# A Mamba-2 scan with an ELU feed-forward block: the second layer from Strassen products to 12-bit words, with the first layer's words kept in DRAM

## The chip, the cores and the metric

The kernel runs on one core of one Trainium2 chip. A core has TensorE (PE; its weight loads are shown as PEld), VectorE (DVE), ScalarE (ACT), GpSimd (POOL) and SyncE (SP, which here only issues transfers). The metric is the device time of one execution in microseconds (us); less is better.

## The reference

A chunked state-space scan gives 3072 rows of 256 values; these go through a feed-forward block of two layers, 256 to 2048 and back, with ELU between them.

```python
batch, n_heads, seq, head_dim, d_state = (4, 8, 768, 32, 16)
...
n_tokens, d_model, d_ff = (3072, 256, 2048)
...
    log_a = np.log(np.clip(a, 1e-06, 1.0))
...
        cum = np.cumsum(la, axis=-1)
        L = np.exp(cum[:, :, :, None] - cum[:, :, None, :])
        L = L * causal
        M = CB * L
        y_intra = np.einsum('bhij,bhjd->bhid', M, xc)
        y_inter = np.einsum('bhin,bhnd->bhid', Cc, state) * decay_to_i[:, :, :, None]
        y[:, :, sl] = y_intra + y_inter
...
    h = x @ w_in
    g = np.where(h > 0.0, h, alpha * (np.exp(np.minimum(h, 0.0)) - 1.0))
    return (g @ w_out).astype(np.float32)
```

The weights `w_in` and `w_out` arrive as 64-bit floats and are turned into 32-bit ones on the chip.

## The kernel before

The 3072 rows are 12 blocks of 256 rows (`BLK`). For each block the scan makes `yT` (the block's rows, transposed), the first layer makes 16 tiles of hidden values, and the second layer sums over these 16 into the block's output. The order of instructions on every engine is the order of the calls in the source (`manual_schedule`); an instruction that waits holds back all that stands behind it on its engine. Semaphores between engines follow from the tiles, and a tile of a pool takes a place that an earlier tile of its tag has left.

Blocks 0 and 1 and a half of the first layer of blocks 2 and 3 are computed with full 32-bit products (`l1` L669, `l2` L854). Everything behind that is done for two blocks at a time: a stage is one round of the loop at L1403 with n = 4, 6, 8, 10 (blocks n and n+1), and the loop at L1322 does the second half of the first layer of blocks 2 and 3. A stage has 16 steps k, one for each tile of 128 hidden values.

The first layer of a step (`l1_words`, L801) works on 12-bit words. Both factors are split into a high word and a rest (`words_of_w` L746, `low_of_w` L756, `words_of_y` L765, `both_of_y` L791), a product of words passes TensorE once per column, and three products give the result: high times high and low times low into `high`, and the product of the sums into `both`. That is six matmuls of 512 columns. ACT then scales `both` into `e` (L818), DVE adds `high` (L826), ACT takes relu and exp (`begin_end`, L832), and DVE writes the hidden values `g` at the beginning of the next step (`end_words`, L839). The words of `w_in` stay in SBUF for the whole run.

The second layer of a pair of blocks lags one stage behind (`second`, L900). It is one level of Strassen's scheme in Winograd's form, with full 32-bit products: seven products instead of eight, in two halves over the hidden dimension. The sums of weights (`weight_steps` L719, `differences` L1267) are made once; the sums of hidden values (`sum_t2` L892 and the `sub` calls on POOL) and the sums of products (`add` on DVE) are made in every stage. `second` is a generator; `l2s(count)` (L1407) draws `count` pieces of two matmuls from it, between the first-layer matmuls of the steps.

The last pair of blocks (10 and 11) has its second layer on words (`late_l2`, L1032): `w_out` is stored to DRAM in 32 bits (`keep_w` L736), read back when the scan's buffers are free (`late_pool` L976) and split, and the hidden values are split, by `jobs`, in the stage n = 10 and behind it. A job has three instructions: ACT takes the high word, DVE the low one, POOL (or DVE in the tail) their difference (`late_words_of_g`, L1000).

The scan of the next pair of blocks runs inside a stage. `stage_scan` (L1383) loads its inputs and makes the decays: `spread_cum` (L387) has loaded the running sums of a block into `L` (128 x 8 x 2 x 64), and `decay_of` (L528) takes, for each head and half, an exponent on ACT with a bias (128x64), 32 for a pair of blocks; after every four heads POOL sets what is above the diagonal to zero (`affine_select`). In step 9 the scores are multiplied with `L` (`weigh` L557) and the states advance (`states` L588), in step 13 the outputs of the scan are made (`across`, `inside`), and at the end of a stage the words of the new `yT` are made ahead of its first step.

PSUM has eight places of one bank: seven of tag "a", and one of tag "o".

Of the kernel before, what the change touches and what calls it, by code (L numbers as in the profile page):

```python
# [23 lines left out]
DIRECT = 4  # L24

# [7 lines left out]
def kernel(  # L33
# [49 lines left out]

    def psum(shape, name):
        return p_a.tile(shape, F32, tag="a", name=name)
# [5 lines left out]
    first = ffn.tile([P, 4, 2, P], F32, tag="c", name="first", bufs=1)  # L91
# [6 lines left out]
    la = const.tile([ROWS, 2, P], F32, name="la")  # L98
# [59 lines left out]
    for i in w_order:  # L158
        w_in[i] = conv.tile([P, KC, CW], F32, tag="w_in", name="w_in", bufs=DF // CW + 1)
    w_out = const.tile([P, MC, DM], F32, name="w_out")  # L160
# [6 lines left out]
    for i in range(MC // 2):  # L167
        pieces.append((
            w_out[:, 2 * i:2 * i + 2],
            w_out64.rearrange("(m p) e -> p m e", p=P)[:, 2 * i:2 * i + 2]))  # L170
    w_raw = {}
    W_AHEAD = 11

    def w_load(i, parts=1):
        if i < len(pieces):
            w_raw[i] = conv.tile([P, 2, 2 * CW], U32, tag="w64", name="w64", bufs=W_AHEAD)
# [8 lines left out]
    w_mag, w_abs_of = {}, {}  # L185
# [4 lines left out]

    def w_abs(i, cols=slice(None)):
        if i in (1, 2) or cols.start:
            w_abs_of[i, cols.start] = psum([P, 2, CW], "ps_mag").bitcast(U32)
        if i not in w_mag:
            w_mag[i] = (ffn.tile([P, 2, CW], U32, tag="tmp", name="mag", bufs=1) if i == 2 else
                        ffn.tile([P, 2, CW], U32, tag="g0", name="mag", bufs=12))
# [17 lines left out]
    w_sgn = {}  # L214

    def w_sign(i, cols=slice(None), eng=nc.vector):
        if i not in w_sgn:
            w_sgn[i] = ffn.tile([P, 2, CW], U32, tag="g1", name="sgn", bufs=12)
# [88 lines left out]
    minus = const.tile([P, P], F32, name="minus")  # L307
# [214 lines left out]

    def decay(n, q):

        decay_of(n, 2 * q)
        decay_of(n, 2 * q + 1)
# [141 lines left out]

    def l1(n, i, parts=1):  # L669
# [22 lines left out]
    def elu():  # L692
        if not begun:
# [4 lines left out]
        g_of[n, i] = ffn.tile([P, 2, BLK], F32, tag=f"g{n % 2}", name="g", bufs=12)  # L698
        nc.vector.scalar_tensor_tensor(
            out=g_of[n, i], in0=e, scalar=1.0, in1=ps,  # L700
# [14 lines left out]
    def sum_weights(eng, a, s, i):  # L715
        for step in weight_steps(eng, a, s, i):
            step()

    def weight_steps(eng, a, s, i):  # L719
        a11, a12, a21, a22 = (part[:, i] for part in a)  # L720
        s2, _, s4 = (part[:, i] for part in s)
        for out, in0, in1, op in (
                (a21, a21, a22, ALU.add), (s2, a21, a11, ALU.subtract), (s4, a12, s2, ALU.subtract)):
            yield lambda: eng.tensor_tensor(out=out, in0=in0, in1=in1, op=op)

    def weight_sums():
        return [conv.tile([P, MC // 2, P], F32, tag="w64", name="w_sum", bufs=W_AHEAD)
                for _ in range(3)]

    w_parts = w_out.rearrange("p (i k) (r c) -> p k r i c", k=2, c=P)  # L730
    a_out = [w_parts[:, k, r] for r in range(2) for k in range(2)]
    s_out = []
    w_kept = tc.dram_tile([P, MC, DM], F32, name="w_kept")
    kept_parts = w_kept.rearrange("p (i k) (r c) -> p k r i c", k=2, c=P)

    def keep_w(k, r):  # L736
        nc.sync.dma_start(out=kept_parts[:, k, r], in_=w_parts[:, k, r])

# [3 lines left out]
    def words_of_w(i):  # L746

        w = pieces[i][0]
        k_words[i] = conv.tile(
            [P, 2, KC, CW], F32R, tag="w64", name="w_words", bufs=W_AHEAD)  # L750
# [5 lines left out]
    def low_of_w(i):  # L756

        w0 = conv.tile([P, KC, CW], F32R, tag="w_in", name="w0", bufs=DF // CW + 1)
# [42 lines left out]
    def l1_words(n, m, ahead=None):  # L801
# [17 lines left out]
        if n == NP - 2 and m > 1:  # L819
            first_of_job()  # L820
# [7 lines left out]
        if n == NP - 2 and m > 1:  # L828
            second_of_job()
# [9 lines left out]
    def end_words():  # L839
        n, m, h, e = late.pop(0)  # L840
        g_of[n, m] = ffn.tile([P, 2, BLK], F32, tag=f"g{m % 2}", name="g", bufs=12)
# [429 lines left out]
    for j in range(2 * DIRECT):  # L1271
# [45 lines left out]
        if j == 3:  # L1317
            s_out[:] = weight_sums()
# [185 lines left out]
```

## Time and profile before

| | us |
|---|---|
| median of 3 runs | 348.37 |
| lowest, highest | 347.66, 348.43 |
| the profiled execution | 348.77 |
| its span, first to last instruction | 347.0 |

The span has these parts, with TensorE's granted clock at 1.00 in all: up to about 20 us the first scan and the first weights; to 82 the blocks 0 and 1 and the 32-bit half of 2 and 3; to about 113 the other half; then the stages n = 4, 6, 8 of some 53 us each; the stage n = 10 up to 320; and the second layer of the last two blocks. HBM was read with 24.61 MB and written with 5.44 MB.

A row of the groups by shape gives line, engine, operation, the tile written and the tiles read, the shape, the count; then the busy time and the mean of one in ns; then the idle time of the engine ahead of them and what ended it. In the chain of waits and the timeline a row begins with the start and the length in us.

### The profile page before, as it was taken

Reading aid. Unit: us, or ns where it says so; the run is one execution under the profiler, and the core shown is the slowest. Engines: PE = TensorE matmul, PEld = TensorE weight load, DVE = VectorE, ACT = ScalarE, POOL = GpSimd, SP = SyncE. Lnnn points to the kernel's source line nnn. Section 1 sums busy time; section 2 is a strip of 40 time slices with the busy share of each in tenths; the row PEclk is TensorE's granted clock in tenths of the full one; section 3 lists DMA queues with packets and bytes.
Section 4 is the critical chain, followed back from the end, with each engine's and each line's share of the span. In section 5 each row is a group of like instructions: output and inputs, shape, how many; then the busy total and the mean of one; then the engine's idle time right before and its main releaser. Section 6 shows DMA issues by size and latency. Waiting matters only on the chain.

```text
span 347.0 us, 9962 instructions
## 1 busy us (share of the span) xinstructions
PE 339.5 (98%) x3902; PEld 297.7 (86%) x3902; DVE 275.3 (79%) x533; ACT 247.7 (71%) x563; POOL 215.8 (62%) x319
## 2 busy tenths in 40 slices
PE   8899999999999999999999999999999999999995
PEld 6569888888788899888889988889988989999995
DVE  3898998889997999866788775788685769898961
ACT  4798989599649988657599547499647487877601
POOL 5553554548999699975196864196954357787200
PEclk9999999999999999999999999999999999999999
DMA  8788999473360660160331070140003500000001
GB/s 146 199 234 177 281 198 257 86 153 97 74 139 2 159 184 23 17 154 4 95 73 30 9 160 5 66 72 2 2 2 89 219 0 3 0 2 30 33 0 62
DMA packets 77208, 30.70 MB, mean 88 GB/s; under 512 B 57897, under 2 KB 71529, under 8 KB 77161
## 3 DMA queue, kind: packets, MB, share of 16 engines
q1 hardware_dynamic: 74984, 29.86, 35.3%
q8 instruction: 31, 0.51, 0.6%
q10 hardware_dynamic: 2176, 0.20, 0.5%
q14 instruction: 17, 0.13, 0.1%
HBM read 24.61 MB, written 5.44 MB: 87 GB/s over the span
## 4 chain that ended last, share of the span: by engine, by line
PE 61%; DVE 12%; ACT 11%; POOL 5%; issue 5%; SPq 2%; DMA 2%; DVEq 0%; ACTq 0%; POOLq 0%
PE ps_o L924 16%; PE ps_h L812 11%; PE ps_h L677 11%; PE ps_o L861 6%; PE ps_w L812 6%; PE ps_both L1042 6%; DVE ps_h L826 4%; ACT e L834 4%; POOL g L877 3%; ACT e L835 3%; DVE y L786 2%; DMA w<-in_moe_w_in_dram 2%; ACT yT L661 2%; DVE M L560 2%; DVE y_both L796 1%
## 5 line engine op out<-in xcount | busy, mean ns | idle before, releaser
L834 ACT ACTIVATE e<-ps_h 128x512 f32<-128x512 f32 x72 | 43.0, 598 | 49.0 <-DVE ps_h L826 49.0
L842 DVE SCALAR_TENSOR_TENSOR g<-e,ps_h 128x512 f32<-128x512 f32 x72 | 49.3, 684 | 30.9 <-ACT e L835 29.1
L924 PEld LDWEIGHTS ps_o<-w_out,g 128*128 128x128 f32 x512 | 64.1, 191 | 5.3 <-ACT p_sum L936 1.1
L924 PE MATMUL ps_o<-w_out,g 128*128 128x128 f32 x512 | 66.3, 276 | 0.6 <-ACT p_sum L936 0.4
L826 DVE SCALAR_TENSOR_TENSOR ps_h<-ps_h,e 128x512 f32<-128x512 f32 x72 | 49.9, 693 | 10.1 <-ACT e L818 8.9
L812 PE MATMUL ps_w<-y_both,w_words 128*128 128x512 f32 x144 | 51.5, 437 | 0.1
L818 ACT ACTIVATE e<-ps_w 128x512 f32<-128x512 f32 x72 | 42.2, 586 | 10.8 <-PE ps_w L812 10.6
L835 ACT ACTIVATE e<-e 128x512 f32<-128x512 f32 x72 | 45.5, 631 | 2.3
L677 PE MATMUL ps_h<-yT,w_in 128*128 128x256 f32 (+1 forms) x208 | 45.2, 368 | 1.9 <-POOL w_in L249 1.9
L812 PE MATMUL ps_h<-y,w_words 128*128 128x512 f32 x144 | 45.6, 398 | 0.0
L877 POOL TENSOR_TENSOR g<-g 128x256 f32<-128x256 f32 x28 | 22.7, 811 | 36.2 <-DVE g L842 36.1
L812 PE MATMUL ps_h<-y,w 128*128 128x512 f32 x144 | 44.9, 392 | 0.0
L677 PEld LDWEIGHTS ps_h<-yT,w_in 128*128 128x128 f32 x208 | 36.3, 190 | 7.7 <-POOL w_in L249 2.8
L531 ACT ACTIVATE L<-L,ncum 128x64 f32<-128x64 f32 x160 | 42.2, 336 | 0.1
L536 POOL TENSOR_SCALAR_AFFINE_SELECT L<-L 64x512 f32<-64x512 f32 x40 | 29.4, 735 | 8.0 <-ACT L L531 6.7
L812 PEld LDWEIGHTS ps_h<-y,w 128*128 128x128 f32 x144 | 27.0, 188 | 7.0 <-POOL w L877 0.4
L924 PE MATMUL ps_o<-w_sum,g 128*128 128x128 f32 x256 | 32.8, 276 | 0.0
L924 PEld LDWEIGHTS ps_o<-w_sum,g 128*128 128x128 f32 x256 | 31.4, 191 | 1.4
L812 PEld LDWEIGHTS ps_h<-y,w_words 128*128 128x128 f32 x144 | 26.6, 188 | 6.1 <-issue 0.4
L861 PE MATMUL ps_o<-w_out,g 128*128 128x256 f32 x128 | 30.4, 381 | 0.0
L861 PEld LDWEIGHTS ps_o<-w_out,g 128*128 128x128 f32 x128 | 24.0, 190 | 3.5
L877 POOL TENSOR_TENSOR g<-t,g 128x256 f32<-128x256 f32 x32 | 23.1, 750 | 4.7 <-PE ps_o L924 4.7
(152 smaller groups left out, 667.4 us busy)
## 6 DMA issues: line engine op xcount, KB each, us to landing
L<-flat SPq DMA_DIRECT2D x20, 256.0 KB
w<-in_moe_w_out_dram SPq DMA_DIRECT2D x8, 512.0 KB
w<-in_moe_w_in_dram SPq DMA_DIRECT2D x7, 512.0 KB
xr<-in_x_dram SPq DMA_DIRECT2D x24, 128.0 KB
w_kept<-w_out SPq DMA_DIRECT2D x4, 512.0 KB
out_dram<-c_sum SPq DMA_DIRECT2D x8, 256.0 KB
w_again<-w_kept SPq DMA_DIRECT2D x4, 512.0 KB
bc<-in_B_dram SPq DMA_DIRECT2D x24, 64.0 KB
```

The source lines that it names most:

```text
L531: nc.scalar.activation(L[:, h, u], L[:, h, u], ACT.Exp, bias=ncum[:, u, row:row + 1])
L536: nc.gpsimd.affine_select(out=part, in_=part, pattern=[[0, 4], [0, 2], [1, Q]], compare_op=ALU.is_ge, fill=0.0, base=0, channel_multiplier=-1)
L677: nc.tensor.matmul(out=ps[:, j, toks], lhsT=w_in[i][:, k, j * P:(j + 1) * P], rhs=yT[n // 2][:, k, n % 2].rearrange("p u i -> p (u i)")[:, ...
L812: nc.tensor.matmul(out=ps, lhsT=lhs[:, k], rhs=rhs[:, k], start=k == 0 and lhs is not w0, stop=k == KC - 1 and lhs is not w1)
L818: nc.scalar.activation(e, both, ACT.Copy, scale=WORD)
L826: nc.vector.scalar_tensor_tensor(out=high, in0=high, scalar=WORD - 1.0, in1=e, op0=ALU.mult, op1=ALU.add)
L834: nc.scalar.activation(e, high, ACT.Relu, scale=-1.0)
L835: nc.scalar.activation(e, e, ACT.Exp, scale=-1.0)
L842: nc.vector.scalar_tensor_tensor(out=g_of[n, m].rearrange("p b i -> p (b i)"), in0=e, scalar=1.0, in1=h, op0=ALU.subtract, op1=ALU.max)
L861: nc.tensor.matmul(out=o_of[n][:, ts], lhsT=g_of[n, j][:, m % 2, ts * P:(ts + 1) * P], rhs=w_out[:, m], start=(m == 0 and ts == 0), stop=( ...
L877: nc.gpsimd.tensor_tensor(out=out, in0=in0, in1=in1, op=ALU.subtract)
L924: nc.tensor.matmul(out=ps[:, ts], lhsT=b[:, ts * P:(ts + 1) * P], rhs=a[:, i], start=(i == chunk[0] and ts == 0), stop=(i == chunk[-1]), s ...
```

## The change

All second layers of blocks 2 to 11 are computed on words, with three products of 256 columns (`three`, `l2_words`). The words of `w_out` are made once, in the second half of blocks 2 and 3 (`words_of_out`, `low_of_out`), and stay in SBUF. The words of `w_in` are stored to DRAM in that half (`keep_words`) and read again in every stage, each of the eight pieces four steps ahead of its use (`load_words`). The hidden values of a stage are split by 16 jobs: at step k the job of piece k+2 gets its ACT instruction (`first_of_jobs`), in step k+1 its DVE and POOL instructions (`rest_of_jobs`), and in step k+2 `l2s(2)` multiplies it, behind the first-layer matmuls of that step. In the stage n = 10 seven more jobs are for the last pair.

The decays of blocks 4 to 11 are made by a sum of 128x1024 on POOL (`decay_sums`), two exponents of 128x512 on ACT (`decay_exps`) and the same four selects on POOL (`decay_mask`) for each block. Nearly all large tiles share two tags, `big` (4 KB a partition, 26 places) and `small` (2 KB, 17 places). `g` has a new layout: one tile holds two tiles of hidden values for both blocks.

The Strassen functions (`second`, `quarters`, `sum_t1`, `sum_t2`, `weight_steps`, `differences`, `store`), `keep_w` and the splitting of `w_out` in the last stage are gone. Cut to its core:

```diff
+    def big(shape, dtype, name):
+        return conv.tile(shape, dtype, tag="big", name=name, bufs=BIG)
+    def small(shape, dtype, name):
+        return conv.tile(shape, dtype, tag="small", name=name, bufs=SMALL)
...
+    def decay_sums(n):
+        L = st[n]["L"]
+        nc.gpsimd.tensor_tensor(
+            out=L, in0=L, in1=ncum[:, :, rows_of(n)].rearrange("p u h -> p h u").unsqueeze(
+                3).to_broadcast([P, NH, 2, Q]), op=ALU.add)
+    def decay_exps(n):
+        L = st[n]["L"]
+        for k in range(2):
+            nc.scalar.activation(L[:, 4 * k:4 * k + 4], L[:, 4 * k:4 * k + 4], ACT.Exp)
...
+    def keep_words(i):
+        words, low = k_words[i]
+        nc.sync.dma_start(out=w_kept[i, :, 0:2], in_=words.bitcast(F32))
+        nc.sync.dma_start(out=w_kept[i, :, 2], in_=low.bitcast(F32))
+    def load_words(i):
+        words, low = big([P, 2, KC, CW], F32, "w_words"), small([P, KC, CW], F32, "w0")
+        nc.sync.dma_start(out=words, in_=w_kept[i, :, 0:2])
+        nc.sync.dma_start(out=low, in_=w_kept[i, :, 2])
...
         nc.scalar.activation(e, both, ACT.Copy, scale=WORD)
-        if n == NP - 2 and m > 1:
-            first_of_job()
+        first_of_jobs()
         if late:
             end_words()
...
         nc.vector.scalar_tensor_tensor(
             out=high, in0=high, scalar=WORD - 1.0, in1=e, op0=ALU.mult, op1=ALU.add)
-        if n == NP - 2 and m > 1:
-            second_of_job()
+        rest_of_jobs()
...
+    def words_of_out(i):
+        w = pieces[DF // CW + i][0]
+        words = big([P, 2, 2, DM], F32R, "o_words")
+        out_words[i] = small([P, 2, DM], F32R, "o_low"), words[:, 0], words[:, 1]
+        nc.scalar.activation(words[:, 0], w, ACT.Copy, scale=NEAR)
+        nc.vector.scalar_tensor_tensor(
+            out=words[:, 1], in0=words[:, 0].bitcast(F32), scalar=1.0 / WORD - 1.0, in1=w,
+            op0=ALU.mult, op1=ALU.add)
+    def low_of_out(i):
+        sub(out_words[i][0], pieces[DF // CW + i][0], out_words[i][1].bitcast(F32))
...
+    def rest_of_jobs():
+        if len(begun_jobs) > 1:
+            for step in range(2):
+                for j in begun_jobs[0]:
+                    next(j)
+            begun_jobs.pop(0)
+    def three(both, high, g, w, first, last):
+        (g1, g0, both_g), (w0, w1, both_w) = g, w
+        for ps, lhs, rhs in ((both, both_g, both_w), (high, g1, w1), (high, g0, w0)):
+            nc.tensor.matmul(
+                out=ps, lhsT=lhs, rhs=rhs, start=lhs is both_g and first > 0 or lhs is g1 and first > 1,
+                stop=last and lhs is not g1, skip_group_check=True)
+    def put_out(row, both, high):
+        eo = small([P, 2, DM], F32, "eo")
+        nc.scalar.activation(eo[:, 0], both, ACT.Copy, scale=WORD)
+        nc.vector.scalar_tensor_tensor(
+            out=eo[:, 1], in0=high, scalar=WORD - 1.0, in1=eo[:, 0], op0=ALU.mult, op1=ALU.add)
+        nc.sync.dma_start(out=out[row:row + P, :], in_=eo[:, 1])
...
+        for step, at in ((decay_sums, (1, 4)), (decay_exps, (2, 5)), (decay_mask, (3, 6))):
+            if k in at:
+                step(m + at.index(k))
...
     for n in range(4, NP, 2):
...
         for k in range(16):
+            if k < 14:
+                to_begin.append(lambda q=k + 2: job(n - 2, q))
+            elif m:
+                to_begin.append(lambda q=k - 14: job(n, q))
+            if not m and k in (4, 6, 8, 10, 12, 14, 15):
+                to_begin.append(lambda q=(4, 6, 8, 10, 12, 14, 15).index(k): late_job(q, late_pool))
             l1_words(n, k, m if k == 15 else None)
             turn_step(n, k // 2 * 2 + 1, k % 2)
+            if k % 2 == 0 and (k > 2 or n > 4) and (k < 12 or m):
+                load_words((k // 2 + 2) % 8)
             if m:
                 stage_scan(n, k)
             begin_end()
             if not m:
-                l2s(4 if k % 2 else 3)
-                third_of_job()
+                l2s(2)
                 continue
-            l2s((3 - (n == 4), 3 - (n == 4), 3, 3, 3, 3, 3, 3, 4, 5, 2, 2, 3, 1, 3, 0)[k])
+            l2s((2 - (n == 4), 2, 2, 2, 2, 2, 2, 2, 2, 2, 1, 1, 2, 1, 1, 0)[k])
```

Here `l2s` draws pieces of six matmuls (one tile of 128 hidden values, both halves of a block's rows, three products), 32 for a pair of blocks. In the scan at the blocks 4 and 5 (`scan_ahead`) the sums, exponents and selects stand in the steps 2 to 6 of the earlier loop.

## The prediction

> **What bounds the kernel now.** I read the page's busy line, the busy time by stage, the chain of waits and one step in order of time, then the groups by shape for the prices.
>
> ```profile
> PE 339.5 (98%) x3902; PEld 297.7 (86%) x3902; DVE 275.3 (79%) x533; ACT 247.7 (71%) x563; POOL 215.8 (62%) x319
> ...
> 221.00:274.00 53.00, 52.72 (x626) 47.16 (x625) 40.05 (x79) 38.29 (x90) 32.26 (x49) 1.00 0.22 64
> 274.00:320.00 46.00, 45.87 (x313) 41.79 (x313) 38.10 (x64) 35.79 (x65) 32.72 (x33) 1.00 0.05 18
> ```
>
> The columns of the lower rows are stretch, length, then PE, PEld, DVE, ACT, POOL busy, the granted clock, the DMA share and GB/s. TensorE is full in every stage at clock 1.00, DVE, ACT and POOL are at 60 to 83%. So a stage costs its matmuls, as long as no matmul waits. The chain shows their pitch:
>
> ```profile
> 234.75 0.93 PE ps_h L812 x4
> 235.68 1.34 PE ps_o L924 x12
> 237.48 0.93 PE ps_h L812 x4
> ...
> 320.41 1.19 PE ps_both L1042 x10
> 321.84 1.20 PE ps_both L1042 x10
> ```
>
> Four first-layer matmuls take 0.93 us (0.2325 each, so 1.40 for the six of a step); 12 records of the Strassen layer (six instructions, each recorded twice) take 1.34. A step is 235.68 to 238.41, 2.73 us. The matmuls on words take 0.12 us each (10 in 1.20). Prices on the other engines:
>
> ```profile
> L826 DVE SCALAR_TENSOR_TENSOR ps_h<-ps_h,e 128x512 f32<-128x512 f32 x72 | 49.9, 693 | 10.1 <-ACT e L818 8.9
> L1006 DVE SCALAR_TENSOR_TENSOR g_low<-g_words,g 128x512 fp32r<-128x512 f32 x16 | 12.5, 788 | 0.0
> L1005 ACT ACTIVATE g_words<-g 128x512 fp32r<-128x512 f32 x16 | 9.5, 622 | 1.9 <-PE ps_high L1042 1.9
> L877 POOL TENSOR_TENSOR g_words<-g_words,g_low 128x512 fp32r<-128x512 f32 x6 | 9.1, 1517 | 2.4 <-ACT e L834 2.4
> L531 ACT ACTIVATE L<-L,ncum 128x64 f32<-128x64 f32 x160 | 42.2, 336 | 0.1
> L536 POOL TENSOR_SCALAR_AFFINE_SELECT L<-L 64x512 f32<-64x512 f32 x40 | 29.4, 735 | 8.0 <-ACT L L531 6.7
> ```
>
> ```profile
> 289.84 1.71 DVE L995 SCALAR_TENSOR_TENSOR w_both<-w_high,w_again 128x512 fp32r<-128x512 f32 x1
> 293.80 0.68 DVE L1006 SCALAR_TENSOR_TENSOR g_low<-g_words,g 128x512 fp32r<-128x512 f32 x1
> ...
> 289.73 1.27 POOL L877 TENSOR_TENSOR g_words<-g_words,g_low 128x512 fp32r<-128x512 f32 x1
> 294.63 1.28 POOL L877 TENSOR_TENSOR g_words<-g_words,g_low 128x512 fp32r<-128x512 f32 x1 [1.65 <-ACT e L834]
> 302.21 1.75 POOL L877 TENSOR_TENSOR g_words<-g_words,g_low 128x512 fp32r<-128x512 f32 x1
> ```
>
> The second block is the timeline (start, us). A word subtraction on POOL takes 1.28 undisturbed and 1.75 beside a DVE instruction with both inputs in SBUF; such a DVE instruction takes 0.68 alone and 1.71 behind a POOL one.
>
> **The change, part by part.** A stage means a pair of blocks (n = 4, 6, 8, 10), step k one l1_words with what follows it.
>
> *TensorE.* Strassen has 7x8x2 = 112 matmuls at 1.34/6 = 0.223, 25.0 us a stage; words have 192 at 0.12, 23.0. Four stages: -8.0.
>
> *Taken from the other engines, per stage.* 19 DVE additions at 0.41 (7.8), 32 POOL subtractions at 0.75 (24); they lie beside matmuls that do not wait, so nothing is won by them alone. ACT loses 32 narrow exponents (pitch 1.06/4, 8.5) for four wide ones (0.55 pitch, 2.2).
>
> *Added, per stage.* 16 jobs: ACT 16x0.62, DVE 16x0.79, POOL 16x1.28; put_out, four ACT at 0.38 and four DVE at 0.42; two sums over 128x1024 on POOL. No row has that shape: 256 elements take 0.73, 512 take 1.28, so 0.55 for each further 256 gives 2.4. Bounds: 1.4 (two one-input selects of 512 at 0.70) and 3.0 (2x1.517); I take 2.4 as it has two inputs. Summed, POOL has 16x1.28+4.8+8x0.70+3.7 (scaled, Sx) = 35 us, DVE about 47, ACT 43: all under 51. By sums alone TensorE stays the bound. The order says otherwise.
>
> *The lead of one step.* The job that step k+1's second layer multiplies gets its DVE part in step k behind the DVE instruction that waits for L1(k), then its POOL part. L1(k) starts at 0; its last matmul starts at 1.16 and ends 0.39 later (a pair shows 0.62), 1.55. DVE "high" from 1.6, "low" from 2.2 (starts are 0.60 apart), done 2.9; POOL starts 0.13 later, 1.28, done 4.3; L2(k+1) from 4.45, 1.44 long; L1(k+2) at 5.9. That is 2.95 a step against 2.73 now and 1.40+1.44 = 2.84 of matmuls.
>
> *The wide exponents in that loop.* At k = 1 and 4 POOL runs the sum right behind the job, at k = 3 and 6 four selects (2.8); at k = 2 and 5 ACT has the two exponents, which wait for the sum, ahead of relu and exp, and behind those stand copy, high, low and the next job. With L2(2) at 0 (its job ended 0.3 before): sum to 2.1, exponents to 3.2, relu and exp to 4.35, DVE end to 4.95, high 5.6, low 6.3, POOL 7.6, L2(4) at 7.75 instead of 5.7. Selects to 10.4, job to 11.7, L2(5) 11.85; second sum to 14.0, exponents 15.15, relu and exp 16.3, end, high, low 18.2, job 19.55, L2(7) 19.7; selects to 22.35, job 23.65, L2(8) 23.8, L2(9) 26.65. Now this stretch takes 19.5 (227.5 to 247.03): +7.2.
>
> *Head and end of a stage.* From the end of L1(15) now to L2(2): y words to +3.85 on DVE, then high, low(0), POOL 6.25, L2(0) 6.4, L2(1) 10.05, L2(2) 12.9; now 10.8: +2.1. (TensorE's filler behind L1(15) shrinks from two rows of 1.78 to three of 0.72, so nothing covers the y words' end.) Behind L2(9): the M products and states (8x0.34+4x0.28) delay high(10) and low(11); L2(11) waits until 10 instead of 8.45, and the rest catches up: 23.4 to the end of L1(15), now 22.3: +1.1. So a stage is +10.4, the -2.0 being inside. Three stages: +31.2.
>
> *Stage n = 10* has no scan: 2.1 at its head, 13 steps at 2.95, 51.1 for 49.3: +1.8. Seven steps carry a second job, whose DVE part goes ahead of the first job's POOL part: between 0.11 each (0.788 less 0.68) and 0.60 each (whole instruction): 0.8 to 4.2, I take 2.5. The Trainium skill's page "SBUF — State Buffer" (Who interferes with whom) says that a DVE instruction with two SBUF inputs and a GpSimd one that reads SBUF hold the shared port for a whole instruction; the 1.71 row agrees, and by that rule this term is 4.2 and the sum 1.7 higher.
>
> *Blocks 2 and 3, second half (82 to 113).* words_of_out puts eight DVE instructions (0.70) and low_of_out eight on POOL there; Strassen's weight sums leave. Cover: TensorE 33.9 of 34, DVE 30.3 of 34 rising to about 32.6. The 16 stores of keep_words (6.3 MB in some 30 us, 210 GB/s on top of 82, against a highest slice of 281) go ahead of the b_tok, L, ec and x loads on SP's queue; the x load is due nine steps later, so 0 to 2 for them. If DVE's cover were gone, its eight instructions are 5.6 and Strassen's four 0.84 are saved: 2.2. Together 0 to +4, taken +1.
>
> *Streaming.* 8 x 768 KB a stage. The four w_again loads (2 MB) moved at 219 GB/s in their slice: 3.6 us for 768 KB, issued four steps (11 us) ahead: hidden by the steps, nothing. SP now issues 16 more in order; what stands behind them (b_tok, L, xr) is due a stage later. The shared tags reuse slots freed at least one step before: nothing. Tail: same matmuls, nothing.
>
> Sum: 31.2+1.8+2.5+1 = 36.5 on the profiled execution's 348.77 (span 347.0 and 1.8 around it), which is 0.4 over the median 348.37: 385.
>
> **Rivals.** (A) TensorE stays full: the jobs' parts finish inside the previous L2, as all sums are under 51. Then only -8.0: 341, faster. For it: TensorE waits for DVE and POOL almost nowhere now. Against: 2.9+0.13+1.28 is over 2.84 even with idle engines; it decides if the POOL part takes under 1.1. The Trainium skill's "Perfetto Trace Analysis" (Identifying the Most-Contended Engine) has one optimize the engine with the highest occupancy first; by that rule this case would win.
> (B) The lead binds, but sums and exponents hide (sum under 1.4, or POOL gets to it earlier): 3x(2.1+1.2+1.1)+1.8+2.5+1 = 18.5, 367. For: POOL is idle for a third of a stage. Against: its order is fixed.
> (C) Streamed words come late: at the span's mean of 87 GB/s the eight loads take 72 us, a stage 19 more than now: over 420. It decides under 100 GB/s. Against: the 219.
> (D) Nothing of it is felt, gains and stalls cancel: within 1 of 348.
>
> **How the numbers follow.** Forecast 0.56, B 0.22, A 0.12, C 0.06, D 0.04. The forecast's own range is 372 to 397: the sum's bounds give -6 and +4, the second job's -2 and +2, the second half -1 and +3, an error of a third in one stage's stalls +-4. The range reaches down to B's lower side, 357, and leaves A, C and D out. Under 0.3% (1 us) this kernel's measurement can't tell a change from none. Faster is A and a part of D, 0.13; same 0.02; slower 0.85.
>
> **What would show it.** In the new profile: TensorE near 88 to 90% of the span and waiting for POOL's g_words in the second layer, most at steps 4, 5, 7 and 8; ACT's wide exponents waiting for POOL about 2 us each; the 128x1024 sum at 2.4; steps of 2.95 in the last stage; w_kept loads that nobody waits for. The forecast is wrong if TensorE waits under 10 us in all, or if most of its waiting is for DMA.

## The result, and the profile after

| | before | after |
|---|---|---|
| median, us | 348.4 | 409.9 |
| lowest, highest | 347.7, 349.7 | 407.9, 410.3 |
| span of the profiled execution | 347.0 | 408.5 |

The ratio is 1.175, with a 95% interval of 1.170 to 1.180: 61 us slower, where the prediction had 36.5. The direction was right, and so was the wait that it named; the size was out of its range, 357 to 397. From the page of the changed kernel, the busy line and the granted clock in 40 slices of the span:

```profile
PE 353.3 (86%) x3774; PEld 294.4 (72%) x3774; DVE 308.1 (75%) x527; ACT 264.8 (65%) x523; POOL 217.4 (53%) x237
...
PEclk9999999977998999999699999989999989999999
```

TensorE has gone from 98% of its span to 86% of a longer one. It has 128 instructions fewer and yet 14 us more of busy time; the second row gives a part of the reason. Some slices have 6, 7 and 8 tenths of the clock; before, it was 1.00 everywhere.

Cutting both spans where the last first-layer matmul of a stage ends (step 15) shows where the time went. The rows are of the changed kernel: stretch, length, then PE, PEld, DVE, ACT, POOL busy, granted clock, DMA share and GB/s.

```profile
75.70:119.20 43.50, 37.02 (x436) 29.75 (x435) 36.72 (x58) 25.00 (x47) 30.71 (x35) 0.88 0.46 140
119.20:190.10 70.90, 56.08 (x592) 46.25 (x591) 54.09 (x85) 45.93 (x86) 45.12 (x44) 0.98 0.50 146
190.10:259.10 69.00, 56.38 (x609) 46.81 (x608) 48.42 (x82) 42.21 (x80) 35.20 (x37) 0.95 0.49 138
259.10:325.10 66.00, 55.05 (x594) 45.74 (x594) 47.87 (x80) 42.47 (x80) 34.92 (x35) 0.97 0.38 117
325.10:380.40 55.30, 51.16 (x295) 41.76 (x293) 41.51 (x63) 42.02 (x77) 29.14 (x22) 0.97 0.30 96
```

| part | before, us | after | longer | predicted |
|---|---|---|---|---|
| second half of blocks 2 and 3 | 34.3 | 43.5 | +9.2 | +1 |
| stage 4 | 53.2 | 70.9 | +17.7 | +10.4 |
| stage 6 | 52.9 | 69.0 | +16.1 | +10.4 |
| stage 8 | 53.0 | 66.0 | +13.0 | +10.4 |
| stage 10 | 49.4 | 55.3 | +5.9 | +4.3 |
| the rest | 28.5 | 28.1 | -0.4 | 0 |

Who waited, from the view of all waits (engine, line, releaser; total us, times, longest):

```profile
POOL g_words L886 <- ACT e L848: 88.0, 38, 7.1
PEld ps_o L959 <- POOL g_words L886: 55.0, 46, 4.3
...
PE ps_o L959 <- POOL g_words L886: 29.8, 31, 3.9
...
ACT L L539 <- POOL L L531: 19.9, 7, 6.1
```

TensorE's second layer (L959) waits for GpSimd's subtraction of a job (L886). GpSimd itself stands idle 88 us in front of these subtractions: it is late because it is fed late, not because it is full. The rows name ScalarE's relu (L848) because it ends last by a hair: ahead of the subtraction at 204.41, it ends at 204.31 and VectorE's low word, which the subtraction really needs, at 204.27. TensorE waits for no streamed load; the list names such a load once, 2.1 us of GpSimd ahead of a subtraction at 168.35 that reads none of its words.

The prediction's walk through this loop came out nearly exact in its times. The starts of the second layer of the steps 2 to 9 in stage 6, from the timeline of TensorE:

```profile
205.77 0.51 PE L959 MATMUL ps_o<-o_words,g_words 128*128 128x256 f32 x2
...
209.95 0.50 PE L959 MATMUL ps_o<-o_words,g_words 128*128 128x256 f32 x2 [1.09 <-POOL g_words L886]
...
213.38 0.50 PE L959 MATMUL ps_o<-o_words,g_words 128*128 128x256 f32 x2 [0.35 <-POOL g_words L886]
...
217.75 0.50 PE L959 MATMUL ps_o<-o_words,g_words 128*128 128x256 f32 x2 [1.28 <-POOL g_words L886]
...
221.77 0.50 PE L959 MATMUL ps_o<-o_words,g_words 128*128 128x256 f32 x2 [0.95 <-POOL g_words L886]
...
225.85 0.51 PE L959 MATMUL ps_o<-o_words,g_words 128*128 128x256 f32 x2 [0.99 <-POOL g_words L886]
...
230.31 0.50 PE L959 MATMUL ps_o<-o_words,g_words 128*128 128x256 f32 x2 [1.37 <-POOL g_words L886]
...
233.23 0.40 PE L959 MATMUL ps_o<-o_words,g_words 128*128 128x256 f32 x2
```

From 205.77 on, L2(4), L2(5), L2(7), L2(8) and L2(9) come at 7.6, 12.0, 20.1, 24.5 and 27.5; the prediction had 7.75, 11.85, 19.7, 23.8 and 26.65. (The first wait comes one step earlier than in the walk, at L2(3).) The whole stretch took 26.9, 27.5 and 27.3 us in the stages 4, 6 and 8, for 19.5, 20.0 and 20.0 before. So the excess lies elsewhere: from the end of the first layer to L2(2), "the head", a stage took 20.2, 15.7, 14.7 and 14.8 us for 10.9, 10.5, 10.8 and 10.8 before, +9.3, +5.2, +3.9 and +3.9 where +2.1 was predicted; and the second half of blocks 2 and 3 took +9.2.

What the heads hide is seen in the windows of 2 us behind the first layer of step 0 in stage 6:

```profile
194.00:196.00 2.00, 0.83 (x2) 0.21 (x2) 1.52 (x3) 1.00 (x2) 0.31 (x1) 1.00 0.00 0
196.00:198.00 2.00, 0.57 (x3) 0.60 (x4) 1.47 (x4) 1.77 (x5) 0.95 (x1) 0.60 0.10 33
198.00:200.00 2.00, 2.00 (x11) 2.00 (x11) 1.83 (x4) 1.23 (x2) 0.78 (x1) 0.50 0.74 160
200.00:202.00 2.00, 2.00 (x7) 1.61 (x7) 0.50 (x1) 0.78 (x2) 0.51 (x1) 0.50 0.76 264
202.00:204.00 2.00, 2.00 (x12) 1.81 (x11) 1.02 (x2) 0.62 (x2) 0.00 (x0) 0.69 0.68 213
```

TensorE is idle for 2.56 us (to 197.43), the granted clock falls to 0.50, and TensorE is then busy without a break but at half speed until 203.2.

### The profile page after: what moved, and what is told of

Same layout as the page of the kernel before. It is cut to its first block, busy times and chain, and to the rows that moved or that the text cites. A ratio compares the mean times of both kernels' runs of the same rounds, so it can differ in the third digit from the quotient of the medians.

```text
span 408.5 us, 9697 instructions
## 1 busy us (share of the span) xinstructions
PE 353.3 (86%) x3774; PEld 294.4 (72%) x3774; DVE 308.1 (75%) x527; ACT 264.8 (65%) x523; POOL 217.4 (53%) x237
## 4 chain that ended last, share of the span: by engine, by line
PE 42%; DVE 20%; POOL 17%; issue 9%; ACT 7%; SPq 2%; DMA 1%; POOLq 0%; DVEq 0%; ACTq 0%
PE ps_o L959 12%; POOL g_words L886 9%; PE ps_h L711 7%; PE ps_h L828 6%; PE ps_both L959 5%; DVE ps_h L841 4%; POOL L L547 4%; PE ps_w L828 4%; DVE g_low L909 3%; PE ps_o L872 3%; DVE M L588 2%; POOL L L531 2%; DVE y L802 2%; PE ps_y L672 2%; DVE y_both L812 1%
## 5 line engine op out<-in xcount | busy, mean ns | idle before, releaser
L886 POOL TENSOR_TENSOR g_words<-g_words,g_low 128x512 fp32r<-128x512 f32 x70 | 93.9, 1345 | 110.0 <-ACT e L848 88.0
L959 PE MATMUL ps_o<-o_words,g_words 128*128 128x256 f32 x512 | 103.2, 298 | 37.9 <-POOL g_words L886 29.8
L959 PEld LDWEIGHTS ps_o<-o_words,g_words 128*128 128x128 f32 x512 | 82.9, 196 | 58.0 <-POOL g_words L886 55.0
L959 PE MATMUL ps_o<-o_low,g_low 128*128 128x256 f32 x256 | 73.6, 287 | 0.0
L848 ACT ACTIVATE e<-ps_h 128x512 f32<-128x512 f32 x72 | 43.0, 597 | 45.1 <-DVE ps_h L841 44.8
L834 ACT ACTIVATE e<-ps_w 128x512 f32<-128x512 f32 x72 | 42.5, 590 | 27.7 <-PE ps_w L828 27.3
L909 DVE SCALAR_TENSOR_TENSOR g_low<-g_words,g 128x512 fp32r<-128x512 f32 x80 | 59.5, 749 | 0.0
L959 PEld LDWEIGHTS ps_o<-o_low,g_low 128*128 128x128 f32 x256 | 50.2, 196 | 0.0
L908 ACT ACTIVATE g_words<-g 128x512 fp32r<-128x512 f32 x80 | 48.5, 624 | 0.0
L872 PE MATMUL ps_o<-w_out,g 128*128 128x256 f32 x128 | 32.4, 399 | 4.9 <-ACT ob L878 4.5
L872 PEld LDWEIGHTS ps_o<-w_out,g 128*128 128x128 f32 x128 | 24.9, 198 | 9.7 <-ACT ob L878 5.1
L828 PEld LDWEIGHTS ps_w<-y_both,w_words 128*128 128x128 f32 x144 | 24.3, 200 | 6.6 <-DVE y_both L812 3.0
```

Of the source, the lines that this page charges most:

```text
L828: nc.tensor.matmul(out=ps, lhsT=lhs[:, k], rhs=rhs[:, k], start=k == 0 and lhs is not w0, stop=k == KC - 1 and lhs is not w1)
L834: nc.scalar.activation(e, both, ACT.Copy, scale=WORD)
L848: nc.scalar.activation(e, high, ACT.Relu, scale=-1.0)
L872: nc.tensor.matmul(out=o_of[n][:, ts], lhsT=g_of[n // 2, j][:, m % 2, n % 2, ts * P:(ts + 1) * P], rhs=w_out[j][:, m % 2], start=(m == 0 a ...
L886: nc.gpsimd.tensor_tensor(out=out, in0=in0, in1=in1, op=ALU.subtract)
L908: yield nc.scalar.activation(words[:, 0], g, ACT.Copy, scale=NEAR / WORD)
```

## The experiments

All times are medians of four executions, beside the kernel before on the same chip; the changed kernel is at 409.9. E2 stands for the end of the first layer of blocks 2 and 3 (119.2 us in the changed kernel, 110.0 before).

### The stretch of the sums: spread, narrow, lead2

**spread** keeps the wide exponents and moves the sums away from them (the helper functions get an argument for a part of the heads):

```diff
-        for step, at in ((decay_sums, (1, 4)), (decay_exps, (2, 5)), (decay_mask, (3, 6))):
-            if k in at:
-                step(m + at.index(k))
-        if k in (7, 8):
-            scaled(m + k - 7, nc.gpsimd)
+        low, high = slice(0, 4), slice(4, 8)
+        for step, j, part in {
+                0: ((decay_sums, 0, low), (decay_sums, 0, high)),
+                2: ((decay_exps, 0, (0, 1)), (decay_mask, 0, (0,))),
+                3: ((decay_mask, 0, (1,)),),
+                4: ((decay_sums, 1, low),),
+                5: ((decay_sums, 1, high),),
+                6: ((decay_exps, 1, (0, 1)), (decay_mask, 1, (0,))),
+                7: ((decay_mask, 1, (1,)),)}.get(k, ()):
+            step(m + j, part)
+        if k in (1, 8):
+            scaled(m + k // 8, nc.gpsimd)
```

> The wide exponents are kept, but each sum runs at least one step before its exponents (first sum at step 0, the second in two halves at 4 and 5), and the selects go two to a step, so ScalarE no longer waits for a sum that stands behind a job. If the waits for the sums are what lengthens the stretch (as in the prediction, 27.3 us from L2(2) to L2(9) in the changed kernel), it falls to seven steps at 2.95 to 3.1, 20.7 to 21.7, three times: 389 to 393 us. Rival: GpSimd is simply too slow for what a step gives it (port, 1.3 a job and 10 us of decays), the order does not matter: the stretch stays above 25 us and the time at 402 to 409.

Measured: 397.0 us (ratio 1.139, 1.136 to 1.143), 12.9 less; stretch 22.6, 22.8 and 22.8 us: between the two ranges, much nearer to the first.

**narrow** undoes the wide exponents in the stages:

```diff
-        for step, at in ((decay_sums, (1, 4)), (decay_exps, (2, 5)), (decay_mask, (3, 6))):
-            if k in at:
-                step(m + at.index(k))
+        for h in range(2 * k - 2, 2 * k) if 0 < k < 9 else ():
+            decay_of(m + h // NH, h % NH)
```

> In the stages 4, 6 and 8 the wide exponents are undone: no sum on GpSimd, four narrow exponents with a bias on ScalarE in each of the steps 1 to 8, as in the kernel before; the selects follow every fourth head. If ScalarE's wait for the sums is what lengthens the stretch, ScalarE's own pitch decides instead, 2.25 for a step's four instructions and 1.06 for four narrow exponents, 3.3 us: stretch 23.1 for 27.3, three times, 396 to 399 us. Rival: ScalarE's time and not the wait is what is short, and 6.3 us more of it a stage make it slower: 410 to 416 us.

Measured: 395.2 us (1.134, 1.133 to 1.136), 14.7 less; stretch 22.4, 22.5 and 22.6 us.

**lead2** begins each job a step earlier:

```diff
-            if k < 14:
-                to_begin.append(lambda q=k + 2: job(n - 2, q))
+            if k < 13:
+                to_begin.append(lambda q=k + 3: job(n - 2, q))
             elif m:
-                to_begin.append(lambda q=k - 14: job(n, q))
+                to_begin.append(lambda q=k - 13: job(n, q))
```

The loop over the second half of blocks 2 and 3 begins its jobs a step earlier in the same way.

> Each job of the second layer is begun one step earlier, so that two steps lie between its first part and its use. If the lead of one step binds, the steps of the last stage fall from 3.0 to 2.84 (3 us there), and in each stage one step of slack takes up part of the waits for sums: stretch 21 to 24 us for 27.3: 391 to 397 us. Rival: ScalarE, waiting in order for the sums, sets the pace and not the lead: stretch above 26, 404 to 409 us.

Measured: 399.8 us (1.147, 1.144 to 1.150), 10.1 less, between the two ranges, and not where it was expected: the stretch is 26.7, 25.5 and 26.4 us, while stage 10 falls from 55.3 to 51.4. Stage 6 gives another 4.9: 1.0 in its head, 2.0 in the stretch and 1.9 at its end. Behind the head of stage 10 TensorE no longer waits at all; from its timeline, the second layer of a step, the first layer, and the second layer of the next:

```profile
344.64 0.40 PE L959 MATMUL ps_o<-o_words,g_words 128*128 128x256 f32 x2
...
346.07 0.63 PE L828 MATMUL ps_w<-y_both,w_words 128*128 128x512 f32 x2
...
347.46 0.40 PE L959 MATMUL ps_o<-o_words,g_words 128*128 128x256 f32 x2
```

A step is 1.43 + 1.39 = 2.82 us, the matmuls alone. The waits of ScalarE's exponents for the sums tell the runs apart; the first line is of spread, the second of lead2 (the changed kernel: 19.9 us, 7 times; narrow has no such sums in its stages):

```profile
ACT L L542 <- POOL L L534: 7.5, 4, 6.1
```

```profile
ACT L L539 <- POOL L L531: 22.7, 7, 6.1
```

One wait of 6.1 us in each of these totals belongs to the blocks 4 and 5, up to 84 us, which none of the three edits touches. In the stages the wait is 13.8 us in the changed kernel, 1.5 in spread and 16.6 in lead2. What follows: in the stages with a scan it is ScalarE, waiting in order for a sum that stands behind a job, which sets the pace; without that wait a step takes 3.2 us, with two quite different ways of making the decays. A longer lead of the jobs helps little there (0.1 to 2.0 us a stage), since the jobs stand behind that wait themselves. Without a scan the lead of one step is the bound. Why a step with a scan still takes 3.2 us and not 2.95 is not shown by these runs.

### The clock: filler

```diff
+            if b == 0 and n > 2:
+                for r in range(20):
+                    nc.tensor.matmul(
+                        out=total[1][:, 0], lhsT=out_words[0][1][:, 0, 0:P], rhs=out_words[0][1][:, 1],
+                        start=True, stop=True, skip_group_check=True)
             for m in range(MC):
```

> Twenty matmuls whose result nothing reads (about 2.3 us) stand ahead of the first second-layer matmul of the stages 6, 8 and 10, where TensorE is idle 2.55 us. If the idle time itself takes the granted clock down (0.62 over 9 us behind it at 195 us, 0.88 over 14 us at 261 and at 328), the clock stays at 1.00 there and the heads get 3.4, 1.7 and 1.7 us shorter: 402 to 405 us, mean clock 0.98. Rival: the clock falls for another reason, or the matmuls are only in the way: 409 to 414 us and the same dips.

Measured: 404.6 us (1.162, 1.158 to 1.166), 5.3 less. The first two rows are from the timeline of TensorE in stage 6, the third is a window of the same place with its columns as above (clock third from the end):

```profile
194.70 2.55 PE L981 MATMUL ps_o<-o_words 128*128 128x256 f32 x20
197.42 0.47 PE L959 MATMUL ps_o<-o_words,g_words 128*128 128x256 f32 x2 [0.17 <-DVE eo L966]
```

```profile
191.00:205.00 14.00, 13.48 (x87) 11.54 (x88) 12.20 (x21) 8.18 (x16) 5.61 (x5) 1.00 0.42 121
```

L2(0) starts at the same moment as before the edit, 197.42 for 197.43: the fillers cost nothing and win nothing by themselves. But the clock stays at 1.00, and the heads of the stages 6, 8 and 10 become 13.5, 13.5 and 13.4 us, all alike, for 15.7, 14.7 and 14.8. That is 4.8 us, and it is shown: the idle time takes the clock down, and the work behind it pays.

The other profiles bear this out. The changed kernel and the eight single edits without filler matmuls have this gap of 2.55 to 2.62 us in 27 heads of the stages 6, 8 and 10. Behind 22 of them the clock is at 0.50 for 3.4 us, and the head takes 14.6 to 14.8; behind four it is so for 6.8 us, and the head takes 15.5 to 15.8; behind one, in stage 10 of late_words, it stays at 1.00, and the head takes 13.3. So the 15.7 of stage 6 is nothing particular to that stage.

### The second half of blocks 2 and 3, and the head of stage 4: ob_big, ahead_narrow, late_words, no_low

In the changed kernel's timeline the copy of block 0's output (ob) waits for GpSimd, TensorE for the copy; the bank of the output is free only then:

```profile
91.42 0.59 ACT L878 COPY ob<-ps_o 128x512 f32<-128x512 f32 x1 [4.32 <-POOL w L886]
...
92.06 3.78 PE L872 MATMUL ps_o<-w_out,g 128*128 128x256 f32 x8 [4.54 <-ACT ob L878]
```

GpSimd's instruction is the low word of a weight piece, which reads the piece whose place of the `small` tag ob is to have. Eight second-layer matmuls then take 3.78 us instead of 1.89: half the clock again, from 87.2 to 97.4. The fall itself comes 0.3 us before this wait begins, behind two waits of TensorE for y_both, 0.99 us to 84.94 and 0.58 to 85.99. In all, TensorE is idle for 6.5 of the 43.5 us of this part (4.5 for ob, 1.6 for y_both, 0.4 for `w_out`) and busy for 37.0, 2.7 more than before the change: that is the whole +9.2.

**ob_big** gives ob a place of the other tag:

```diff
-            ob = small([P, 2, DM], F32, "ob")
+            ob = big([P, 2, DM], F32, "ob")
```

> The copy of the first output block (ob) takes a place of the larger tag, so that it no longer waits for the low word of a weight piece on GpSimd. If this wait, with the half clock behind it, is the main part of the 9.2 us lost before stage 4 (TensorE idle 4.5 us at 87.5 to 92, then 0.50 of the clock to 97), the time falls by 6 to 9 us: 401 to 404. Rival: GpSimd's and VectorE's queues of weight words are what is late there and the wait moves to the next tile: 407 to 410.

Measured: 405.0 us (1.162, 1.159 to 1.165), 5.0 less, between the two ranges; E2 at 115.9. The wait falls to 0.2 us and the clock is 1.00 up to 98.7, where 3.4 us at 0.50 follow; of 9.2 us 5.9 stay. (In spread, narrow and filler, which leave this part alone, E2 lies between 118.4 and 119.5.)

**ahead_narrow** makes the decays of blocks 4 and 5 with narrow exponents:

```diff
-        for step, at in ((decay_sums, (2, 4)), (decay_exps, (3, 5)), (decay_mask, (3, 6))):
-            if i in at:
-                step(m + at.index(i))
+        for q in {2: (0,), 3: (1, 2), 4: (3,), 5: (4, 5), 6: (6,), 7: (7,)}.get(i, ()):
+            decay(m + q // 4, q % 4)
```

> The wide exponents are undone for blocks 4 and 5 alone, whose decays are made while blocks 2 and 3 run: no 128x1024 sum on GpSimd (2.4 us at 81.9) ahead of the low words of pieces 4 and 5, and 32 narrow exponents on ScalarE in six steps as in the kernel before. If this sum is what makes the low words late, and with them the copy of ob (TensorE idle 4.5 us) and the half clock behind it, 4 to 8 us go before stage 4: 402 to 406. Rival: the selects and the low words themselves hold GpSimd, and ScalarE gets 6 us more to do there: 409 to 413.

Measured: 406.0 us (1.163, 1.155 to 1.171), 4.0 less; E2 at 116.1. The waits for y_both are gone, and the wait for ob is still 3.4 us, so the sum is a part of its cause and not the whole.

**late_words** moves the last words of weights into stage 4 (`words_of_w(3)` and `words_of_out(7)` are taken out of step 15 of the loop before it):

```diff
     end_words()
-    low_of_w(3)
-    keep_words(3)
-    low_of_out(6)
-    low_of_out(7)
...
+            if n == 4 and k == 1:
+                low_of_out(6)
+            if n == 4 and k == 2:
+                words_of_w(3)
+                low_of_w(3)
+                keep_words(3)
+            if n == 4 and k == 4:
+                words_of_out(7)
+                low_of_out(7)
```

> The words of the last first-layer piece (3), of the last second-layer piece (7) and the low word of piece 6 are made in steps 1 to 4 of stage 4 instead of ahead of it, where VectorE gives them 1.76 and 1.77 us and GpSimd 5.7 us between the first and the second job. If these queues are what lengthens the head of stage 4 (20.2 us from the end of the first layer to L2(2), the other heads 14.7 to 15.7), the idle 3.5 us at 133 goes, and 4 to 6 us with it: 403 to 406 us. Rival: they are in the way wherever they stand: 408 to 411.

Measured: 407.5 us (1.169, 1.166 to 1.172): 2.4 less, with an interval that overlaps that of the changed kernel. L2(1) of stage 4 comes at 133.4 for 136.5, but the stretch behind it takes 29.1 us for 26.9. What is won at the head is lost again in the steps. Of the 2.4 us 1.5 are in stage 10, where the clock happens not to fall in this profile.

**no_low** leaves GpSimd's low words out, but for piece 4, whose words are stored as soon as they are made (`keep_words(4)` moves to stand behind `low_of_w(4)`):

```diff
     def low_of_w(i):
+        if i != 4:
+            w0 = small([P, KC, CW], F32, "w0")
+            nc.sync.dma_start(out=w0, in_=w_kept[4, :, 2])
+            k_words[i] = k_words[i], w0.bitcast(F32R)
+            return
...
-        out_words[i] = small([P, 2, DM], F32R, "o_low"), words[:, 0], words[:, 1]
+        low = small([P, 2, DM], F32, "o_low")
+        nc.sync.dma_start(out=low, in_=w_kept[4, :, 2])
+        out_words[i] = low.bitcast(F32R), words[:, 0], words[:, 1]
...
     def low_of_out(i):
-        sub(out_words[i][0], pieces[DF // CW + i][0], out_words[i][1].bitcast(F32))
+        pass
```

> GpSimd makes the low word of piece 4 only; the low words of the other seven first-layer and of all eight second-layer pieces are filled by a DMA of piece 4's instead, so this part of the computation is left out. If GpSimd's 15 low words (28 us of it from 82 to 135) are what lengthens the second half and the head of stage 4, by slowing VectorE's words of the same time (1.11 and 1.15 us instead of 0.68) and by standing ahead of the copy of ob and of the first jobs, VectorE's words fall to 0.68 to 0.75 and the time by 9 to 14 us: 396 to 401. Rival: the words' own number on VectorE and ScalarE is what is late, with or without GpSimd: 404 to 409.

Measured: 401.8 us (1.153, 1.146 to 1.159), 8.2 less, a little less than was expected. The groups of VectorE's words, first of the changed kernel between 82 and 135 us (with GpSimd's low words beside them), then of this run between 75 and 135:

```profile
L886 POOL TENSOR_TENSOR o_low<-w_out,o_words 128x512 fp32r<-128x512 f32 x8 | 12.0, 1501 | 3.6 <-DMA out_dram<-ob 3.6
L896 DVE SCALAR_TENSOR_TENSOR o_words<-o_words,w_out 128x512 fp32r<-128x512 f32 x8 | 9.2, 1150 | 0.0
L768 DVE SCALAR_TENSOR_TENSOR w_words<-w_words,w_in 128x512 fp32r<-128x512 f32 x8 | 8.9, 1113 | 0.0
```

```profile
L768 DVE SCALAR_TENSOR_TENSOR w_words<-w_words,w_in 128x512 fp32r<-128x512 f32 x8 | 5.7, 717 | 0.0
L903 DVE SCALAR_TENSOR_TENSOR o_words<-o_words,w_out 128x512 fp32r<-128x512 f32 x8 | 5.5, 682 | 0.0
```

The same 16 instructions take 11.2 us instead of 18.1 when GpSimd is not at the same work. The head of stage 4 falls from 20.2 to 14.3 us, about what the other heads take; its waits of 3.9 us at 126.8 and 3.5 at 136.5 become 1.3 and 2.0, and the clock no longer falls there. But E2 (120.1) does not get earlier: ob now waits 2.4 us for VectorE's words of the same piece, which stand behind y_both and work of the scan there, half the clock follows as before, and TensorE waits 1.1 us for the fills that the edit itself adds.

### The stream: twice

```diff
         nc.sync.dma_start(out=low, in_=w_kept[i, :, 2])
+        again = tc.dram_tile([P, 3, KC, CW], F32, name="again")
+        nc.sync.dma_start(out=again, in_=w_kept[i])
```

> Each load of a streamed piece is followed by a copy of the same 768 KB from DRAM to DRAM, so the traffic of the stream is more than doubled (28 copies, 22 MB read and 22 MB written). If the stream is hidden with time to spare, as predicted, nothing changes: 408 to 411 us. Rival: the loads are near to being late: 415 us and more.

Measured: 413.1 us (1.186, 1.182 to 1.189), 3.2 more: neither theory. TensorE waits for no load. Gaps of another kind have grown, here in the timeline of TensorE of this run ("issue": it waited for nothing that the profile shows):

```profile
320.71 0.81 PE L672 MATMUL ps_y<-M,xr 64*32 64x64 f32 x58
324.28 0.31 PE L672 MATMUL ps_y<-M,xr 64*32 64x64 f32 x6 [2.76 <-issue]
```

Such gaps make 4.5 us here, 2.2 in the changed kernel (1.63 of them in stage 6), and none of 0.2 us or more between 70 and 330 us before the change. They differ from profile to profile, though: in the other single edits, with the same stream as the changed kernel, those among these small matmuls make 0.3 to 1.0 us. The head of stage 4 is longer too in this profile, 22.6 us, with the clock at 0.50 from 135.0 to 141.9. So the cost of the traffic is measured, and its path is not shown.

### Together: combo4, best, best2

**combo4** is spread, lead2, ob_big and filler.

> The four edits of the first runs together (sums spread, jobs a step earlier, ob in the larger tag, filler matmuls). If they take away different waits, their gains add: 12.9 + 10.1 + 5.0 + 5.3 = 33 us, 376 to 379. If the sums and the lead of one step are one loop, as in the prediction's walk, spreading and earlier jobs take away partly the same waits: 381 to 387 us.

Measured: 382.6 us (1.097, 1.095 to 1.099), 27.3 less, where the single gains add to 33.3. A new wait came: L2(8) for the copy of the output block, 2.7 us in each of the stages 6 and 8, behind an exponent that waited for its sum. These 5.4 us are nearly what is missing, so it is not shown that spread and lead2 take partly the same waits away, though the time lies in the range of that theory.

**best** adds late_words and orders the decays again, with whole sums in place of spread's halves:

```diff
+        for step, at in ((decay_sums, (0, 3)), (decay_exps, (1, 5))):
+            if k in at:
+                step(m + at.index(k))
+        for j, h, at in ((0, 0, 2), (0, 1, 4), (1, 0, 6), (1, 1, 7)):
+            if k == at:
+                decay_mask(m + j, (h,))
```

> The four edits and the late words together, with the decays in another order: whole sums at steps 0 and 3, exponents at 1 and 5, two selects each at 2, 4, 6 and 7. In the four edits together ScalarE still waited up to 2.6 us for a sum at step 6, and the copy of the output block behind it held TensorE for 2.7 us at L2(8), with a lower clock behind it, in each of three stages. If this is the late sum's doing, 3 to 4 us a stage and 2.5 from the late words go: 366 to 371 us. Rival: the wait comes from the one bank that the output blocks share and stays: 376 to 381. Neither theory gives less than 350.

Measured: 379.5 us (1.088, 1.084 to 1.092). The wait at L2(8) falls to 0.7 us, so it was mostly the late sum's doing, although the time lies in the range of the rival; stage 10 is at 49.8 (49.4 before the change). But in stage 4, where the late words now stand in the steps, TensorE waits 5.3 us for jobs; the stage still takes 65.9 (65.7 in combo4), and the gain is about a quarter of what was expected.

**best2** adds ahead_narrow.

> The last combination with the decays of blocks 4 and 5 on narrow exponents too. With ob in the larger tag the wait for its place is gone already, so only the 1.6 us of waits for y_both at 85 to 87 and what the sum delays behind them are left to win: 375 to 378 us. Rival: ScalarE's narrow exponents cost there what GpSimd saves: 379 to 383.

Measured: 377.1 us (1.080, 1.077 to 1.084). None of these beats the kernel before. In best, most of the 31 us left are 6.7 in the second half of blocks 2 and 3, 12.7 in stage 4, 5.7 each in the stages 6 and 8. TensorE is busy for 92% of that span; the words' matmuls are cheaper, but the 2.0 us that they save in a stage are less than what the idle time and the steps of 3.2 us take.

## Why the prediction was right and wrong

**The matmuls** were priced rightly: six of the first layer 1.39 (1.40), twelve on words 1.43 (1.44). The gain of 8.0 is in the result, under the waits. **The sums of the engines** came out as worked out: in stage 6 GpSimd, VectorE and ScalarE are busy 35.2, 48.4 and 42.2 us (35, 47 and 43). The prediction was right not to stop there, as rival A did: TensorE had the highest share, got less work, and the time rose. The Trainium skill's "Perfetto Trace Analysis" (Identifying the Most-Contended Engine) has one optimize the engine with the highest occupancy first. Here that engine, TensorE at 98%, got 8.0 us less to do, and the highest share did not say what bounds the changed kernel.

**The lead of one step** is shown in the stage without a scan: 13 steps of stage 10 took 40.7 us (seven of 2.9 to 3.1, six of 3.2 to 3.4), predicted 13 at 2.95 and 2.5 for the second jobs, 40.9; with two steps of lead a step falls to 2.82. By the lock rule of the Trainium skill's "SBUF — State Buffer" (Who interferes with whom) that term was 4.2 and the sum 42.6; the runs lie with the smaller.

**The wide exponents in that loop** are shown: +7.2 a stage was predicted, +7.4 measured, and both ways of taking the wait away win 4.2 to 4.9 us a stage in the stretch. That the total fits so well is in part luck. By the prediction's own rival B the lead has 1.2 of the 7.2 and the exponents 6.0; without their wait the stretch is still 2.6 to 3.1 us longer than before the change, so the exponents' part was put too high and the rest too low. GpSimd's sum took 1.94 to 2.39, for 2.4. TensorE waited at the steps 3 to 8, not most at 4, 5, 7 and 8. Rival B, sums that hide, lay 18 us under the forecast; spread and narrow, which make it so, lie 13 and 15 under the changed kernel.

**The head of a stage, +2.1, is the step that failed first**, by 1.8 to 7.2 us a stage. The prediction read "clock 1.00" off the old profile and carried it into a kernel that has TensorE idle 2.55 us behind step 0. The filler shows what that cost: 4.8 us in three heads. With the clock at 1.00 a head is 13.5, which is +2.6 to +3.0, so the walk itself was off by 0.5 to 0.9: it left out the copy of the last output block (`put_out`, eo), for which L2(0) waits in the filler run too; L2(0) comes 7.3 us behind the end of L1(15), for 6.4. Stage 4 has a head of its own, which the prediction priced like the others: there VectorE's and GpSimd's words of weights stand ahead of the first jobs and slow each other; without GpSimd's low words 5.9 of its 20.2 us go.

**The second half of blocks 2 and 3, +1, is the other**, at +9.2. The prediction looked for the cost in the added work: eight instructions on VectorE at 0.70, which it found covered, and eight on GpSimd, to which it gave no time. The cost lay in waits that it put at nothing or left out. The shared tags were to reuse slots "freed at least one step before: nothing"; instead the place of ob makes TensorE wait 4.5 us, with half the clock around it, and the wide sum of blocks 4 and 5, which has no term, delays y_both and ob. ob_big and ahead_narrow take 3.3 and 3.1 us off E2; some 3 us of the 9.2 are taken away by neither.

The price of the words was wrong too: VectorE's 16 took 1.13 and GpSimd's eight 1.50 beside each other. Such a price had been put to the last stage, from the 1.71 row, but not here. The rule of the Trainium skill's "SBUF — State Buffer" (Who interferes with whom) that was weighed there, one lock for a VectorE instruction with two inputs in SBUF and a GpSimd one that reads SBUF, fits: 18.1 us of VectorE with, 11.2 without. But without it E2 stays at 120.1, so it is only in the head of stage 4 that GpSimd's low words are shown to cost time. Whether they do it by slowing VectorE or by standing ahead of the jobs on GpSimd, no run separates.

**The ends of the stages** took +1.1, +3.4 and +1.8 for +1.1; 1.6 of stage 6 is an issue gap. **Streaming** was hidden as predicted as far as waits for loads go, and rival C falls; more than twice the traffic costs 3.2 us, so more of it would not be quite free. **The tail** is unchanged. In sum: stretches, ends and stage 10 from its L2(2) on 27.1 predicted and 30.5 measured, the four heads 8.4 and 22.3, the second half 1 and 9.2.

## What to carry to other kernels

The granted clock of a kernel whose TensorE never waits cannot be carried over to a change that makes it wait. Here gaps of some 2.55 us were paid twice in 26 heads of 27, so price the matmuls behind every new gap at the lower clock, or fill the gap. Before an instruction is moved to an engine with room, look at who waits for it in order: a sum that ScalarE must wait for at the front of its queue holds everything behind it, at any share of busy time. Where VectorE and GpSimd are both to make words from SBUF, take their price from a row in which they run together. And when tiles get a shared tag, look up which instruction must end before each place is free.

## What the runs showed of the hardware

**The clock falls and rises on a fixed grid.** In the changed kernel it is at 0.50 from 87.2 to 97.4, 128.1 to 131.5, 196.4 to 203.2, 268.1 to 271.5 and 332.9 to 336.3 us: lengths of 10.2, 3.4, 6.8, 3.4 and 3.4, and the starts lie 40.9, 68.3, 71.7 and 64.8 apart, all near whole multiples of 3.41. The fall at 268.1 came 1.5 us after a gap of 2.55 us had ended. The Trainium skill's "TensorE: Matmul & The Clock Gate" (What's actually happening) describes free-running windows of 3413 ns; the trace agrees. Its rule of no idle gaps over some 3.4 us (HAM oscillation — how this bites in real kernels) does not fit: gaps of 2.55 us were followed by half the clock three times, and one of 3.46 us (133.0 to 136.5) was not. In the filler run the same gap, 3.58 us up to 136.1, was followed by it, from 137.7 to 141.1: whether a gap is paid for differs between profiles of the same stretch.

**TensorE can stand idle where the profile shows nothing to wait for.** The issue gaps stand among 64 small matmuls in a row. During the one of 1.63 us up to 254.9 transfers moved 353 GB/s, during the one of 0.53 up to 321.3 none. They made 2.2 us in the changed kernel, 4.5 with the traffic of twice and 0.3 to 1.0 in the other single edits. What makes them is not shown; that the fetching of instructions waits behind data is a guess that no run here tests.
